# Fifty-six offsets in the last part of a list scheduler's order: soft-capped attention followed by a mixture of attention experts

## The chip, the core and the metric

The kernel runs on one core of a Trainium2 chip. A core has five engines that run side by side, each with its own in-order stream of instructions: TensorE (PE in the profile: matrix products and transposes, with weight loads shown apart as PEld), VectorE (DVE), ScalarE (ACT), GpSimd (POOL) and SyncE (SP), which here issues nearly all DMAs. Sixteen DMA engines move data between the device memory and the on-chip buffer. TensorE writes into eight banks of accumulators; the other engines read results from there. The metric is the device time of one execution in microseconds; the figure given for a kernel is the median of its runs.

## The reference

The first stage is attention for 8 batches and 12 heads, with 448 positions and a head size of 64, whose scores are capped by a tanh:

```python
scores = scale * np.matmul(q, k.transpose(0, 1, 3, 2))
scores = cap * np.tanh(scores / cap)
attn = softmax(scores)
x = (attn @ v) with heads merged        # 8 x 448 x 768
```

The second stage is a layer of four experts, each of them a causal attention with a head of size 64. A gate picks two of the four for every position:

```python
logits = x @ w_gate
w = softmax over the two largest logits
for e in range(4):
    q, k, v = x @ wq[e], x @ wk[e], x @ wv[e]
    a = softmax(causal(scale * q @ k.T))
    out += (weight of e at this position) * (a @ v @ wo[e])
```

The output is 8 x 448 x 768 in 32-bit floats.

## The kernel before

The first stage goes by pairs of heads: 48 pairs, six to a batch, and two more groups (numbers 48 and 49) that hold the last 128 query rows of the last batch for three pairs each. For each pair, TensorE turns q and k around, forms the scores in a left group of three banks (X) and a right group of two (Y), ScalarE takes tanh from there in three pieces (line 854) and then the exponential in place (line 866). TensorE multiplies the result with v (lines 881 and 889), VectorE normalises (lines 910 and 913), and the result is turned around into the tile xT, by TensorE for the early pairs and by a transposing DMA (line 400) for later ones.

The second stage for a batch runs while the first stage of the next batch goes on. Its parts, by the names that the scheduler gives them:

- `v6_n` (line 1003): values and gate logits of batch 6 for four blocks of 128 rows; `k6_r`, `q6_r` (line 1011): its keys and queries for two pairs of experts.
- The gate: a chain of small GpSimd operations on the logits, which ends in masks `mB6` that a DMA turns around into `mT`. VectorE multiplies the queries by them (`qm6`, line 1085).
- `sB6_s` (line 1207): the causal scores of the s-th chosen expert, 18 products in seven pieces; ScalarE takes their exponential (`eB6_s`, line 1216), GpSimd cuts the diagonal blocks (line 1226).
- `pvB6_s` (line 1266): scores times values, for four row blocks; VectorE scales them into `oB` (line 1281), GpSimd adds the two choices (line 1291), DMAs turn the sum around into `oT`, and `wo6` (line 1328) multiplies by the output weights, in two halves per row block. A copy by VectorE or ScalarE (line 388) puts each half into an output tile `ob`, and SP stores it (line 1342) when both halves are there.

Batch 7 has nothing to hide behind. Its first 320 rows are done by `last` (lines 1431 to 1513) and its last 128 rows by `last2` (lines 1593 to 1651): products of halves that were begun earlier (`hkL`, `hqL`), the other halves (`kL`, `qL`, line 1443), values (`vL`, `cvL`, line 1476), scores (`sL..`, line 1495, and `sR.`, line 1624), products with the values (`pvL0` to `pvL2`, line 1533, and `pvL3`, line 1651), normalisation (lines 1357 to 1365), transposes (`oTL`, line 1372), output products (`woL`, line 1394), copies into the tiles `kf`, and five stores (lines 1403, 1409 and 1412). Two of the last stores are issued by ScalarE's queue, the others by SP.

None of this order is written out. The kernel first records every operation in a graph, with an engine, an estimated duration and what it reads and writes. `dues` gives each operation a due time, worked back from the fixed sequence of ScalarE's tanh and exponential operations. `solve` then is a list scheduler: at each step it finds, for each engine, the operation that can start first by the estimates, and among those that can start at about that moment it takes the one with the smallest rank. The rank is the due time plus some corrections:

```python
d = u.due + lag if u.first or left < TAIL else max(u.due + lag, t0 + 0.0)
d -= 7.653 * (u.grp is not None and not u.opens and left >= TAIL)
```

A table of seeds, one for each 4 us of the planner's time, adds a small pseudo-random shift. Banks are given out in the same pass, so another order also means other banks. After that the operations are issued engine by engine in the order found; at run time each engine works through its list in order, and waits where an input or a bank isn't ready. An operation that may run on VectorE or ScalarE (`alt`) is placed on either only when the fixed ScalarE sequence is over.

Of the kernel before, what the change touches and what calls it, by code (L numbers as in the profile page):

```python
# [21 lines left out]
FLIGHT = 8  # L22
JIT = 1.798
SEEDS = (0, 0, 110, 0, 0, 306, 0, 782, 317, 0, 303, 0, 680, 715, 825, 0, 899, 21, 0, 595, 84, 0, 0, 430, 634, 477, 0, 0, 952, 0, 477, 0, 829, 206, 468, 485, 0, 0, 522, 517, 134, 0, 182, 0, 903, 141, 149, 0, 334, 0, 875, 527, 0, 0, 667, 121, 852, 28, 0, 742, 969, 79, 85, 225, 0, 0, 0, 500, 463, 0, 0, 356, 833, 724, 418, 803, 322, 931)
TWIRE = 0.1
BEGIN = {"POOL": 0.8, "DVE": 0.9, "SP": 0.8, "ACT": 0.8, "PE": 1.25}
NWARM = 6
# [31 lines left out]
class Graph:  # L59
# [79 lines left out]
    def solve(self, when, banks, lent):  # L139
        free = dict(BEGIN)  # L140
        sent = []
        ready = {}
        at = {}
        bank_at = {b: 0.0 for b in (*banks, *lent)}
        taken = {b: [o for o in self.ops if b in o.takes] for b in lent}
        for o in self.ops:
            o.nd = len(o.deps)
            if o.grp is not None:
                o.grp.bank = None
            if o.nd == 0:  # L150
                ready.setdefault(o.eng, []).append(o)
                at[o.idx] = 0.0
        order = []
        n = len(self.ops)
        left = sum(o.fixed for o in self.ops)
        half = 0
        lag = 0.0
        wire = 0.0

        def pick(o, t):  # L160
            best = None
            for b in o.grp.banks:
                s = max(t, bank_at[b])
                if s >= INF:
                    continue
                if b in taken and taken[b]:
                    continue
                if best is None or s < best[0]:
                    best = (s, b)
            return best or (INF, None)  # L170

        def est(o, e):
            t = max(free.get(e, 0.0), at[o.idx])
            if o.opens:
                t = pick(o, t)[0]
            for b in o.takes:
                t = max(t, bank_at[b])
            if (e == "SP" or o.wire) and len(sent) >= FLIGHT:
                t = max(t, sent[-FLIGHT])
            if e == "PE" and o.half != half:  # L180
                t = max(t, free.get(e, 0.0) + SWITCH)
            return t

        while len(order) < n:
            best = None
            for e, rs in ready.items():
                if not rs:
                    continue
                c = [(est(o, e), o) for o in rs if e == o.eng or not left]
                if not c:  # L190
                    continue
                t0 = min(x[0] for x in c)
                if t0 >= INF or (best is not None and t0 >= best[0]):
                    continue
                def rank(x):
                    u = x[1]
                    if u.name[:4] == "gexp":
                        return -INF, 0.0, 0
                    d = u.due + lag if u.first or left < TAIL else max(u.due + lag, t0 + 0.0)
                    d -= 7.653 * (u.grp is not None and not u.opens and left >= TAIL)  # L200
                    k = SEEDS[int(t0 / 4.0)] if t0 < 4.0 * len(SEEDS) else 0
                    if k:
                        d += ((u.idx * 40503 + k * 9973) % 1009 / 1009.0 - 0.5) * JIT
                    return d - 5.546 * (u.half == 1 and half == 1), u.due, u.idx

                near = t0 + (0.085 if left >= TAIL else SWITCH + 0.02)
                t, o = min((x for x in c if x[0] <= near), key=rank)
                early = e == "POOL" and t < HEAD
                if (e in ("PE", "DVE") or early) and not o.first:
                    for t2, u in c:  # L210
                        if u.first and u.due + lag < t + o.occ + 0.517 and t2 < t + (
                                o.occ if early else max(SWITCH + 0.01, min(o.occ, 0.25))):
                            t, o = t2, u
                            break
                if best is None or t < best[0]:
                    best = (t, e, o)
            assert best is not None, "stuck"
            t, e, o = best
            ready[o.eng].remove(o)
            if o.alt:  # L220
                ready[o.alt[0]].remove(o)
                if e != o.eng:
                    o.eng, o.occ, o.lat = o.alt
            left -= o.fixed
            o.start = t
            if e == "PE" and t < WARM:
                o.lat = 2.0 * o.base
                free[e] = t + 2.0 * o.base
                o.lat += 0.165
            else:  # L230
                free[e] = t + o.occ
            if o.wire:
                wire = max(wire, t + (LAND if t > 3.0 else LAND0)) + o.wire
                o.lat = wire - t + (0.35 if t > 3.0 else 0.0)
            if o.eng == "SP" or o.wire:
                sent.append(t + o.lat)
            if e == "PE":
                half = o.half
            if o.idx in when:
                lag = t - when[o.idx]  # L240
            if o.opens:
                b = pick(o, t)[1]
                o.grp.bank = b
                bank_at[b] = INF
            for b in o.takes:
                bank_at[b] = INF
                if b in taken:
                    taken[b].remove(o)
            if o.closes:
                bank_at[o.grp.bank] = t + o.lat + SEM  # L250
            for b in o.frees:
                bank_at[b] = t + o.lat + SEM
            order.append(o)
            for s, late in o.succ:
                at[s.idx] = max(at.get(s.idx, 0.0), t + self.gap(o, s, late))
                s.nd -= 1
                if s.nd == 0:
                    ready.setdefault(s.eng, []).append(s)
                    if s.alt:
                        ready.setdefault(s.alt[0], []).append(s)  # L260
        return order
# [19 lines left out]
def kernel(  # L281
# [116 lines left out]
    def turned(n, dst, src, r, w, name, due=None):  # L398

        sp(lambda: nc.sync.dma_start_transpose(  # L400
            dst().rearrange("p (n t) -> p n t", t=128), src()), r, w, due, name,
           wire=TWIRE * n, occ=1.25)

# [1385 lines left out]
```

## Time and profile before

| | |
|---|---|
| time, median of 3 runs | 304.8 us (304.11 to 304.95) |
| profiled execution: span | 303.4 us |
| difference of the median to that span | 1.4 us |
| busy share of PE / DVE / ACT / POOL | 93% / 72% / 96% / 61% |
| instructions in the profile | 8986 |

The profiler gives the profiled execution as a span, from its first to its last instruction; a time of its own beside the span is not given, so the median of the runs stands for it. Busy time of TensorE is modelled, since its products are pipelined: the step from one product's start to the next one's is a better measure of what it costs than its listed duration. In a view in order of time each line has the start, the duration, the engine, the line of the kernel, the operation, what it writes and reads, and how many alike are merged; square brackets hold idle time ahead of it and what ended that. A "q" behind an engine's name is its queue, where DMAs are issued.

### The profile page before, as it was taken

How to read it: one execution, taken by the hardware profiler on the slowest of the kernel's cores; microseconds unless marked ns; L12 is line 12 of the kernel's file. 1: busy time of each engine (PE TensorE's matmuls, PEld its weight loads, DVE VectorE, ACT ScalarE, POOL GpSimd, SP SyncE). 2: the span in 40 equal slices, each digit the busy share in tenths (PEclk: the TensorE clock that was granted, in tenths of full speed). 3: DMA queues.
4: the chain of work that ended last, by engine and by line, in shares of the span. 5: the costliest groups of instructions: out<-in, count | busy, mean ns of one | idle time of the engine just before them, and what ended most of it. 6: DMA issues, size and time to landing. Idle time of an engine off the chain costs nothing.

```text
span 303.4 us, 8986 instructions
## 1 busy us (share of the span) xinstructions
PE 281.0 (93%) x3488; PEld 187.7 (62%) x3488; DVE 218.2 (72%) x653; ACT 290.8 (96%) x247; POOL 184.7 (61%) x515
## 2 busy tenths in 40 slices
PE   7779789899999999999999999999999999999993
PEld 3445546477665776667675776557566565676861
DVE  3336558577877878597877877788777758678993
ACT  5999999999999999999999999999999999999792
POOL 6793433998699684958589553945569212940340
PEclk9999999999999999999999999999999999999998
DMA  6789979999971999568997972178026730433327
GB/s 192 181 200 292 238 200 274 259 256 224 251 168 56 283 269 248 144 180 251 228 245 139 269 218 81 37 140 235 3 55 130 216 79 2 94 75 127 98 88 278
DMA packets 86875, 53.13 MB, mean 175 GB/s; under 512 B 47536, under 2 KB 83120, under 8 KB 86832
## 3 DMA queue, kind: packets, MB, share of 16 engines
q1 hardware_dynamic: 86448, 52.13, 68.1%
q8 instruction: 27, 0.44, 0.6%
q10 hardware_dynamic: 384, 0.43, 0.4%
q14 instruction: 16, 0.13, 0.2%
HBM read 36.19 MB, written 11.01 MB: 156 GB/s over the span
## 4 chain that ended last, share of the span: by engine, by line
ACT 59%; PE 30%; issue 3%; DMA 3%; DVE 2%; SPq 1%; POOL 1%; POOLq 0%; ACTq 0%
ACT yp L854 29%; ACT yp L866 25%; PE A L1011 4%; ACT pP L1216 4%; PE A L889 3%; PE Y L801 3%; PE A L1328 3%; DMA kf<-in_k_dram 2%; PE A L1003 2%; PE A L1266 2%; PE A L881 2%; PE X L1207 1%; PE A L934 1%; PE X L801 1%; DMA oT<-oS 1%
## 5 line engine op out<-in xcount | busy, mean ns | idle before, releaser
L866 ACT ACTIVATE yp<-yp 128x3136 f16<-128x3136 f16 (+4 forms) x51 | 141.1, 2769 | 0.0
L854 ACT ACTIVATE yp<-Y 128x896 f16<-128x896 f32 (+2 forms) x100 | 99.2, 992 | 1.2 <-PE Y L801 1.2
L854 ACT ACTIVATE yp<-X 128x1344 f16<-128x1344 f32 (+2 forms) x50 | 67.1, 1343 | 0.6 <-PE X L801 0.4
L889 PE MATMUL A<-v,yp 128*128 128x65 f16 x1116 | 55.4, 193 | 0.0
L889 PEld LDWEIGHTS <-yp 128*128 128x128 f16 x1116 | 48.4, 97 | 3.7 <-issue 1.5
L881 PE MATMUL A<-vtz,yp 128*128 128x130 f16 x186 | 41.2, 222 | 4.4 <-ACT yp L866 2.7
L913 DVE TENSOR_TENSOR xk<-A,rca 128x256 f16<-128x256 f32 x96 | 39.9, 415 | 3.2
L691 POOL CAST v<-vf 128x384 f16<-128x384 f32 x48 | 24.0, 507 | 16.9 <-PE A L889 12.8
L655 POOL CAST q<-qf 112x512 f16<-112x512 f32 x44 | 26.7, 616 | 10.8 <-PE A L705 6.2
L764 DVE COPY qk<-A 128x960 f16<-128x960 f16 x32 | 20.5, 655 | 12.1 <-PE A L705 11.7
L881 PEld LDWEIGHTS <-yp 128*128 128x128 f16 x186 | 18.0, 97 | 17.8 <-issue 8.5
L388 DVE COPY ob<-A 128x384 f32<-128x384 f32 (+1 forms) x48 | 25.2, 551 | 4.7 <-PE A L1328 4.3
L910 DVE RECIPROCAL rca<-A 128x4 f32<-128x4 f32 x96 | 17.0, 178 | 15.3 <-PE A L889 13.9
L801 PE MATMUL Y<-qk 64*128 64x448 f16 x136 | 24.7, 358 | 2.3 <-ACT yp L854 1.4
L1281 DVE SCALAR_TENSOR_TENSOR oB<-A,rcb,mw 128x256 f16<-128x256 f32 x53 | 24.9, 480 | 1.8
L1266 PE MATMUL A<-vB,pP 128*128 128x260 f16 x132 | 22.5, 274 | 1.7 <-DVE oB L1281 1.6
L1328 PE MATMUL A<-wo,oT 128*128 128x384 f16 x98 | 22.4, 325 | 1.0 <-DMA oT<-oS 0.5
L1291 POOL TENSOR_TENSOR oS<-oB,oB 128x512 f16<-128x512 f16 x14 | 16.0, 1153 | 10.6 <-issue 9.5
L1003 PE MATMUL A<-wvg,xT 128*128 128x260 f16 x168 | 22.1, 274 | 0.4 <-DVE vB L999 0.3
L705 PE MATMUL A<-ident,q 112*128 112x112 f16 x192 | 19.9, 213 | 1.2 <-POOL q L655 1.1
L640 POOL CAST k<-kf 128x384 f16<-128x384 f32 x33 | 16.3, 509 | 6.3 <-DMA kf<-in_k_dram 3.1
L1226 POOL TENSOR_SCALAR_AFFINE_SELECT pP<-pP 128x384 f16<-128x384 f16 x14 | 7.4, 525 | 20.6 <-ACT pP L1216 20.6
(240 smaller groups left out, 598.7 us busy)
## 6 DMA issues: line engine op xcount, KB each, us to landing
qf<-in_q_dram SPq DMA_DIRECT2D x23, 448.0 KB, 6.0
kf<-in_k_dram SPq DMA_DIRECT2D x23, 384.0 KB, 4.9
vf<-in_v_dram SPq DMA_DIRECT2D x23, 384.0 KB, 5.2
out_dram<-ob SPq DMA_DIRECT2D x21, 384.0 KB, 3.3
ktf<-in_k_dram SPq DMA_DIRECT2D x46, 32.0 KB, 4.8
vtf<-in_v_dram SPq DMA_DIRECT2D x46, 32.0 KB, 4.8
out_dram<-ob SPq DMA_DIRECT2D x6, 192.0 KB, 2.9
ob<-in_moe_wv_dram SPq DMA_DIRECT2D x2, 384.0 KB, 4.9
```

Of the source, the lines that this page charges most:

```text
L388: (nc.scalar.copy if o.eng == "ACT" else nc.vector.tensor_copy)(dst(), src())
L655: e(q16[i], qf[s][:, h].rearrange("p h (c d) -> p c h d", c=QC))
L801: nc.tensor.matmul(dst[:, g, o], kT[r, 128 * (c + 1) : 128 * (c + 2)], t[r, qs], start=True, stop=True,)
L854: ACTS[what, p] = act(c_act(n * (b - a)), lambda: nc.scalar.activation(y[:, a:b, 0:n], src[:, 0 : b - a, 0:n], AF.Tanh, scale=isc / capf), ...
L866: act(c_act(n * (b - a), False), lambda a=a, b=b, n=n: nc.scalar.activation(y[:, a:b, 0:n], y[:, a:b, 0:n], AF.Exp, scale=capf), ks, ks, f ...
L881: nc.tensor.matmul(ps[:, n, :, :], y[:, 2 * S + w : 2 * S + w + 128], vtz[u], start=(n == 0), stop=False, skip_group_check=True,)
L889: nc.tensor.matmul(ps[:, n, h, :], y[:, o : o + 128], v16[u][:, h, c, :], start=False, stop=(c == 2), skip_group_check=True,)
L913: dve(c_dve(128 * m), lambda g=g, i=i, rc=rc, m=m: nc.vector.tensor_tensor(xk[p % NXK][:, 2 * i : 2 * i + m, :, :], view(g)[:, 0:m, :, 0:D ...
L1003: nc.tensor.matmul(bank(g)[:, 0 : E * Dh + E], xT[x][:, j, WIN[n] : WIN[n] + 128], wvg[:, j, :], start=(j == j1), stop=(j == jn),)
L1266: nc.tensor.matmul(bank(g)[:, 0 : E * (Dh + 1)], pB[pi][:, o : o + 128], vB[x][:, c, :, :], start=(t == 0), stop=(t == len(cs) - 1),)
L1281: dve(c_dve(E * Dh) + 0.06, lambda g=g, k_=k_, n=n: nc.vector.scalar_tensor_tensor(oB[s][:, n, :, :], view(g)[:, :, 0:Dh], rcb[k_][:, 0, : ...
L1328: nc.tensor.matmul(bank(g)[:, 0 : D // 2], oT[x][:, n // 2, r, n % 2, :], wo2[r][:, c0:c1], start=(r == 0), stop=(r == 1),)
```

## The change

A table gives 56 operations, named by their number in the graph, an offset in hundredths of a microsecond. From 249.5 us of the planner's time on, the offset is added to the operation's rank; a positive one lets others go first. Nothing else is changed.

```diff
+RANKS = (
+    (249.5, {
+        2260: -386, 2303: -114, 2314: 197, 2330: 2378, 2341: 324, 2348: 3565, 2372: 3326, 2399:
+        -428, 2401: -1930, 2484: 214, 2490: -459, 2508: 5066, 2519: 291, 2526: -4288, 2529:
+        -162, 2566: 232, 2568: 1338, 2569: -246, 2575: 354, 2583: 806, 2586: 1059, 2591: 749,
+        2593: 434, 2604: 113, 2607: 115, 2608: 79, 2632: 192, 2647: 153, 2648: 2441, 2655: 1463,
+        2663: 275, 2665: -730, 2678: 187, 2680: 644, 2689: 2077, 2692: -456, 2694: 1630, 2695:
+        6618, 2696: -2260, 2724: 343, 2725: 98, 2729: 835, 2732: -33, 2734: 418, 2739: 765,
+        2744: 384, 2746: -1204, 2768: 842, 2773: 182, 2774: 799, 2784: 320, 2787: 206, 2789:
+        767, 2794: 829, 2802: 704, 2807: -322,
+    }),
+)
...
                     d = u.due + lag if u.first or left < TAIL else max(u.due + lag, t0 + 0.0)
                     d -= 7.653 * (u.grp is not None and not u.opens and left >= TAIL)
+                    for since, table in RANKS:
+                        if t0 >= since:
+                            d += table.get(u.idx, 0) / 100
```

The numbers that matter below: 2330 is the start of `k6_0` and 2348 of `q6_1`; 2372 is a row block of `pvB5_1`; 2508 is the fourth of the seven pieces of the scores `sB6_0`; 2526 is a row block of `pvB6_0`; 2583, 2586, 2591 and 2593 are halves of the output products `wo6` (2583 is the second half of row block 0); 2689 and 2692 are value blocks `vL`; 2695 and 2696 are the value block `cvL`; 2746 is a transpose `oTL`.

What the offsets do to the order, from the listing of both programs: up to the planner's 249.5 us all engines' lists are the same. Behind that, `k6_0` moves behind `q6_0`; the logits and values `v6_0` move from the last place of four to the third; three `wo5` halves and most of `pvB6` move ahead; the seven pieces of `sB6_0` are split after the third, with two groups of pair 44 and a block of `pvB5_1` between. In the last part two of the four score blocks `sL..` move ahead of the last attention groups, the two value blocks `vL` change places, and the last row blocks' products are interleaved. The last nine stores, seven of them on SP, come there in the order ob0, ob2, kf0, ob1, kf2, kf1, kf3 instead of ob0, ob1, ob2, kf0, kf3, kf1, kf2 (kf2 and kf3 have a second half on ScalarE's queue).

## The prediction

> **What bounds the kernel now.** I read the page's totals, then the chain that ended last, then each engine in order of time over the last 50 us (the change acts from 249.5 us of the planner's time), then the stretches of the end with their DMA share.
>
> ```profile
> span 303.4 us, 8986 instructions
> PE 281.0 (93%) x3488; PEld 187.7 (62%) x3488; DVE 218.2 (72%) x653; ACT 290.8 (96%) x247; POOL 184.7 (61%) x515
> ```
>
> ScalarE carries the kernel: tanh and exp stand back to back. The part that the change touches, by stretch (busy us of each engine with its count, then granted clock, DMA share, GB/s):
>
> ```profile
> core 0: us, PE busy (x) PEld busy (x) DVE busy (x) ACT busy (x) POOL busy (x), PEclk, DMA share, GB/s
> 265.00:275.00 10.00, 9.39 (x143) 7.16 (x142) 7.96 (x28) 9.62 (x10) 4.03 (x13) 1.00 0.47 135
> 284.90:290.00 5.10, 5.07 (x78) 3.87 (x76) 4.75 (x22) 2.65 (x10) 1.06 (x2) 1.00 0.23 51
> ```
>
> Until 284.9 us ScalarE sets the pace, with TensorE nearly as full; behind it ScalarE is half idle, and TensorE and VectorE carry a chain of small products and copies. Then come the stores. The same view, cut finer at the end:
>
> ```profile
> 293.80:294.80 1.00, 1.00 (x15) 0.75 (x15) 0.86 (x4) 0.70 (x4) 0.54 (x2) 1.00 0.95 378
> 294.80:295.20 0.40, 0.40 (x4) 0.12 (x3) 0.40 (x2) 0.40 (x3) 0.00 (x0) 1.00 0.18 69
> 295.20:296.00 0.80, 0.80 (x17) 0.66 (x16) 0.73 (x4) 0.80 (x3) 0.00 (x0) 1.00 1.04 422
> 299.00:300.00 1.00, 0.00 (x0) 0.00 (x0) 0.00 (x0) 0.09 (x1) 0.00 (x0) 1.00 1.04 409
> 300.00:301.00 1.00, 0.00 (x0) 0.00 (x0) 0.00 (x0) 0.00 (x0) 0.00 (x0) 1.00 0.88 215
> 293.80:302.00 8.20, 4.75 (x47) 2.71 (x46) 4.47 (x15) 3.73 (x10) 0.54 (x2) 0.99 0.92 336
> 302.00:303.40 1.40, 0.00 (x0) 0.00 (x0) 0.00 (x0) 0.00 (x0) 0.00 (x0) 0.50 0.00 0
> ```
>
> This is the reading on which the forecast turns. From 293.8 to 302.0 the 16 DMA engines are busy 0.92 of the time: 8.20 x 0.92 = 7.54 us of transfers, with one real hole at 294.8 to 295.2. So the end is set by a queue of stores that never empties, and the last copy only decides when the last piece joins it. The stores, by issue and by size:
>
> ```profile
> 292.94 2.68 SPq L1342 DMA_DIRECT2D out_dram<-ob  x3
> 296.05 0.33 SPq L1412 DMA_DIRECT2D out_dram<-kf  x1
> 299.12 0.53 ACTq L1409 DMA_DIRECT2D out_dram<-kf  x1
> out_dram<-ob SPq DMA_DIRECT2D x3, 384.0 KB, 2.8
> out_dram<-kf SPq DMA_DIRECT2D x2, 384.0 KB, 3.3
> out_dram<-kf ACTq DMA_DIRECT2D x2, 192.0 KB, 3.0
> out_dram<-kf SPq DMA_DIRECT2D x2, 192.0 KB, 2.8
> ```
>
> Nine stores, 5 x 384 + 4 x 192 = 2688 KB, all issued between 292.94 and 299.12. The first data move 0.86 us after the first issue (293.80 - 292.94), and 1.36 us pass from the last data (302.0) to the end of the span. So the span is 292.94 + 0.86 + 8.20 + 1.36 = 303.36. The median of the runs, 304.8, is 1.4 us above the span; I carry that difference over unchanged.
>
> **The change, part by part.** No operation is added or taken away; 56 offsets change which ready operation the planner takes. Listing both programs by engine, the first difference stands at TensorE's blocks for pair 42; from there the counts are the same but for one copy that goes from ScalarE to VectorE.
>
> *Scores of expert block 6 (offset +50.66 on the fourth of their seven pieces).* Before, all 18 products stand together and end just as ScalarE gets free; ScalarE then loses 0.38 us once, behind a wait of TensorE for a transposing DMA:
>
> ```profile
> 265.25 1.08 PE L1207 MATMUL X<-qm,kB 128*128 128x64 f16 x18
> 266.72 0.22 PE L881 MATMUL A<-vtz,yp 128*128 128x130 f16 x1
> 266.96 0.22 PE L881 MATMUL A<-vtz,yp 128*128 128x130 f16 x1
> 267.20 0.49 PE L1266 MATMUL A<-vB,pP 128*128 128x260 f16 x3
> 269.00 0.82 PE L1328 MATMUL A<-wo,oT 128*128 128x384 f16 x4 [0.47 <-DMA oT<-oS]
> 266.44 1.07 ACT L1216 ACTIVATE pP<-X 128x1024 f16<-128x1024 f32 x1
> 273.40 1.13 ACT L854 ACTIVATE yp<-X 128x1152 f16<-128x1152 f32 x1 [0.38 <-PE X L801]
> ```
>
> In the new order two attention groups (0.24 each, 266.72 to 266.96) and three L1266 products (0.11 each) stand between the pieces: 0.48 + 0.33 = 0.81 us later, less some 0.25 by which TensorE gets there earlier, since the two blocks of the q products no longer wait behind the late k block. ScalarE waits 0.56 us there. In return the waits of 0.47 and 0.38 should go: in the new program the sum L1291 that feeds this oT stands ahead of part of the gate work on GpSimd, the logits that start the gate chain come one block earlier, and so SP's queue (masks, xT, oT, in the same order) moves up. The price of a transpose that lands later is bounded by nothing and by the 3.34 us of this row of the chain, against 2.3 to 2.4 for most of its kind:
>
> ```profile
> 265.62 3.34 DMA oT<-oS
> ```
>
> At 3.34 us it would still land before its products. Sum for ScalarE's chain: +0.56 - 0.38 = +0.2, less for work that closes up later; I take +0.1, between -0.4 (no wait at the scores) and +0.6 (the waits stay).
>
> *The tail: the first store.* From the last attention group of TensorE to the second product of output block 0, which completes the first store, it is 291.29 - 285.29 = 6.00 us:
>
> ```profile
> 285.29 0.22 PE L960 MATMUL X1s<-vtz,yp 128*128 128x130 f16 x1
> ...
> 285.53 0.28 PE L1593 MATMUL A<-xT,wq 128*128 128x128 f16 x2
> 285.64 0.28 PE L1593 MATMUL A<-xT,wk 128*128 128x128 f16 x2
> ...
> 287.45 0.31 PE L1495 MATMUL X2s<-qB,kB 64*128 64x320 f16 x1
> ...
> 287.73 0.27 PE L1593 MATMUL A<-xT,wk 128*128 128x128 f16 x2
> ...
> 291.05 0.25 PE L1495 MATMUL A<-qB,kB 64*128 64x192 f16 x1
> ...
> 291.29 0.50 PE L1328 MATMUL X1s<-wo,oT 128*128 128x384 f16 x2
> ...
> 292.18 0.48 PE L1328 MATMUL X2s<-wo,oT 128*128 128x384 f16 x2
> 292.50 0.29 PE L1533 MATMUL A<-vB,pP 128*128 128x65 f16 x4
> 292.36 0.55 DVE L388 COPY ob<-X1s 128x384 f32<-128x384 f32 x1
> ```
>
> In the new order that product comes later: ahead of it now stand two more L1328 pairs (0.32 each, 292.18 to 292.50), the 24 products of L1533 (four take 0.13 up to the next group, so 0.78) a score block (0.24, 291.05 to 291.29) and two pairs of 128 columns (0.11 each, 285.53 to 285.64), while two score blocks (0.28, 287.45 to 287.73, and 0.24) have moved ahead of the start and four changes between half-height and full-height products go (some 0.1 each). That is 0.64 + 0.78 + 0.24 + 0.22 - 0.52 - 0.40 = +0.96. Its copy stood 1.07 us after it (292.36 - 291.29), behind other VectorE work; the shortest this can be is the product's own 0.50 and a little more, about 0.62. I take 0.45 off, since fewer gate operations stand there, and 0.1 for a pair that leaves the start. First store: +0.1 + 0.96 - 0.45 - 0.1 = +0.5, bounded by 0 and +1.4; I take +0.4.
>
> *The tail: the last store.* ScalarE waits twice for TensorE ahead of its last copies:
>
> ```profile
> 297.77 0.48 ACT L388 COPY kf<-X1s 128x384 f32<-128x384 f32 x1 [0.61 <-PE X1s L1394]
> 298.61 0.48 ACT L388 COPY kf<-A 128x384 f32<-128x384 f32 x1 [0.37 <-PE A L1394]
> ```
>
> In the new order the products of all four last blocks are interleaved, so that one block's copies run beside another's products; the two waits, 0.98 us, go, and about half a microsecond of TensorE's own waits with them. The last issue should go from 299.12 to some 297.6, an estimate between no gain and 2 us. It does not enter the sum, because what stands behind it is the queue of stores.
>
> *The drain.* 7.54 us of transfers stay, since the bytes do. The hole at 294.8 to 295.2 (0.4 x 0.82 = 0.33) goes: in the new SP order the second store stands right behind the first with its copies done. Of the 0.12 lost in 300.0 to 301.0 I count all; the ramp at both ends stays. So the drain is 8.20 - 0.45 = 7.75, bounded by 7.54 and 8.20.
>
> [...] The rows show SP and ACT stores drawing on the same busy share (1.04 at 299 to 300, with a store of ACT's queue issued at 299.12). [...]
>
> *Sum.* +0.4 (first store) - 0.45 (drain) = -0.05 us: a span of 303.3, and 304.7 us beside the median of 304.8.
>
> **The rivals.** *Faster: the stores give way too.* For it: the tail work does end about 1.5 us earlier, and the stretch at 300 to 301 moves only 215 GB/s at a share of 0.88; if this half-rate store overlaps with others instead of standing at the end, 0.45 goes. With that, and the first store no later than now: -0.45 - 0.45 = -0.9, 303.9; with ScalarE's chain 0.4 earlier as well, 303.5, which I take as its time. Without any sharing of engines it would be the last issue 1.5 earlier, 303.3. Against it: 2688 KB at the 400 GB/s of the full rows need most of 7 us, whatever the order.
>
> *Slower: VectorE's queue before the first store.* VectorE is busy 4.75 of 5.10 us there and gains a copy (0.55). If the copy of the second half of block 0 again stands 1.07 us behind its product, and the row of normalisations that now comes earlier costs two more copies (2 x 0.55) ahead of it, the first store is 0.4 + 0.45 + 1.1 = 1.95 later and the time is 304.8 + 1.95 - 0.45 = 306.3. It decides once that copy starts more than 1.35 us after the present 292.36. For it: the store needs both halves, and SP's queue is in order, so everything waits behind it. Against it: VectorE's gate chain for the last rows, which held the copy until 292.36, moves up.
>
> *The waits at the scores stay and grow:* ScalarE +0.6, first store +0.9, 305.3. This lies within the range. That the table does nothing is excluded by the listing of the new program.
>
> **How the numbers follow.** A measurement of this kernel can tell about 0.3% (0.9 us) from no change. Forecast (within that) 0.57, with the 305.3 of the grown waits counted there; faster 0.25; slower by VectorE's queue 0.18. The predicted time is 304.7. The range goes from 303.5, the faster rival's own time, to 305.7, half way into the slower one; about 0.1 is left out on each side.
>
> **What would show it.** Right: the first store of ob at 293.2 to 293.5, the last store issued before 298, a DMA share near 1.0 from about 294.2 with no hole, data until about 302; ScalarE with a gap of about 0.5 ahead of the L1216 exp near 266.9 and none of 0.38 at 273; no TensorE wait for oT. Wrong: if data end before 301.2, the stores do not set the end as I read them; if the first store is later than 294, the order of the copies is at fault; a TensorE wait for mT or oT beyond 0.5 us would shift all of it.

## The result, and the profile after

The changed kernel takes 306.83 us (median of 9 runs, 306.56 to 308.84) beside 304.8 us of the kernel before (9 runs on the same chip): a ratio of 1.0063, with a 95% interval of 1.0034 to 1.0091. It is slower by about 2 us, where 304.7 us and no change were forecast.

Line numbers of the new kernel are 15 higher (L1216 is now L1231). The page's totals, after:

```profile
span 305.4 us, 8987 instructions
PE 281.7 (92%) x3488; PEld 188.4 (62%) x3488; DVE 219.0 (72%) x654; ACT 290.6 (95%) x246; POOL 184.6 (60%) x515
```

The busy times move by 0.8 us at most, so most of the 2.0 us between the two spans is idle time. The stretches of the end (busy us of each engine with its count, then granted clock, DMA share, GB/s):

```profile
265.00:275.00 10.00, 9.96 (x147) 7.37 (x144) 8.80 (x29) 9.62 (x11) 3.14 (x9) 1.00 0.56 123
...
293.80:294.80 1.00, 1.00 (x18) 0.74 (x18) 0.97 (x4) 0.95 (x3) 0.41 (x1) 1.00 0.00 0
294.80:296.00 1.20, 1.20 (x17) 0.88 (x14) 0.94 (x5) 1.05 (x3) 0.00 (x0) 1.00 0.76 307
297.00:298.00 1.00, 0.92 (x6) 0.32 (x4) 0.90 (x3) 0.50 (x3) 0.00 (x0) 1.00 1.05 411
299.00:300.00 1.00, 0.00 (x0) 0.00 (x0) 0.00 (x0) 0.00 (x0) 0.00 (x0) 1.00 0.98 224
300.00:301.00 1.00, 0.00 (x0) 0.00 (x0) 0.00 (x0) 0.00 (x0) 0.00 (x0) 1.00 1.03 332
302.00:303.00 1.00, 0.00 (x0) 0.00 (x0) 0.00 (x0) 0.00 (x0) 0.00 (x0) 0.63 0.61 226
303.00:304.00 1.00, 0.00 (x0) 0.00 (x0) 0.00 (x0) 0.00 (x0) 0.00 (x0) 0.50 0.10 35
295.10:304.06 8.96, 2.82 (x21) 1.36 (x18) 2.92 (x8) 2.29 (x6) 0.00 (x0) 0.90 0.86 308
```

The first row is for later. The others show three things. Data start 1.30 us later (295.10, before 293.80). At 299 to 300 the DMA engines are all busy, yet move only 224 GB/s. And the end is ragged: from 302 on the share falls to 0.61 and 0.10: some of the 16 engines have finished and others have not. In the kernel before, the last stretch with data was this, and nothing came behind it:

```profile
301.00:302.00 1.00, 0.00 (x0) 0.00 (x0) 0.00 (x0) 0.00 (x0) 0.00 (x0) 0.91 0.74 246
```

The stores of the kernel after, in order of issue:

```profile
294.25 0.83 SPq L1357 DMA_DIRECT2D out_dram<-ob  x2
295.33 0.33 SPq L1427 DMA_DIRECT2D out_dram<-kf  x1
296.26 0.33 SPq L1357 DMA_DIRECT2D out_dram<-ob  x1
297.24 0.49 SPq L1424 DMA_DIRECT2D out_dram<-kf  x1
297.24 0.52 ACTq L1424 DMA_DIRECT2D out_dram<-kf  x1
297.93 0.67 SPq L1427 DMA_DIRECT2D out_dram<-kf  x1
298.47 0.71 ACTq L1418 DMA_DIRECT2D out_dram<-kf  x1
298.69 1.10 SPq L1418 DMA_DIRECT2D out_dram<-kf  x1
```

The last store is issued 0.43 us earlier than before (298.69, before 299.12), but the span ends 6.7 us behind it where it was 4.2. The two stores of L1424 have 64 rows each, half of the 128 partitions. They ended the queues before; now they stand in the middle.

One more difference must be taken out before the two profiles are compared. The engines' lists are the same up to the first exp of expert block 5, and there the new profile is already 0.31 us late. In order of time, the kernel before and then the kernel after:

```profile
243.50 1.18 ACT L1216 ACTIVATE pP<-X 128x1024 f16<-128x1024 f32 x1
```

```profile
243.81 1.17 ACT L1231 ACTIVATE pP<-X 128x1024 f16<-128x1024 f32 x1
```

In the profiles of the experiments this row comes between 242.51 and 246.35, and where I followed it back it arose in the first 30 us of an execution. So below every trace is read from that exp on: from it to the end of the last instruction it is 59.86 us in the kernel before and 61.55 after, a difference of 1.69.

### The profile page after: what moved, and what is told of

Read it like the earlier page. It is cut to its first block, busy times and chain, and to the rows that moved or that the text cites. A ratio compares the mean times of both kernels' runs of the same rounds, so it can differ in the third digit from the quotient of the medians.

```text
span 305.4 us, 8987 instructions
## 1 busy us (share of the span) xinstructions
PE 281.7 (92%) x3488; PEld 188.4 (62%) x3488; DVE 219.0 (72%) x654; ACT 290.6 (95%) x246; POOL 184.6 (60%) x515
## 4 chain that ended last, share of the span: by engine, by line
ACT 56%; PE 33%; DVE 3%; issue 3%; DMA 1%; ACTq 0%; POOL 0%; DVEq 0%; POOLq 0%
ACT yp L869 28%; ACT yp L881 24%; PE A L1026 4%; PE A L904 4%; ACT pP L1231 4%; PE Y L816 4%; PE A L1343 3%; PE A L896 2%; PE A L1018 2%; PE A L1281 2%; PE X L1222 2%; PE X L816 1%; PE A L949 1%; DMA ktf<-in_k_dram 1%; DVE xk L928 1%
## 5 line engine op out<-in xcount | busy, mean ns | idle before, releaser
L928 DVE TENSOR_TENSOR xk<-A,rca 128x256 f16<-128x256 f32 (+1 forms) x96 | 39.8, 416 | 3.2
L925 DVE RECIPROCAL rca<-A 128x4 f32<-128x4 f32 (+1 forms) x96 | 17.1, 178 | 15.7 <-PE A L904 14.4
L1343 PE MATMUL A<-wo,oT 128*128 128x384 f16 x102 | 23.4, 326 | 0.5 <-DVE qm L1100 0.4
```

The source lines that it names most:

```text
L928: dve(c_dve(128 * m), lambda g=g, i=i, rc=rc, m=m: nc.vector.tensor_tensor(xk[p % NXK][:, 2 * i : 2 * i + m, :, :], view(g)[:, 0:m, :, 0:D ...
L1343: nc.tensor.matmul(bank(g)[:, 0 : D // 2], oT[x][:, n // 2, r, n % 2, :], wo2[r][:, c0:c1], start=(r == 0), stop=(r == 1),)
```

## The experiments

All results together. "From the exp" is the time from the first exp of block 5; the drain runs from the first to the last data of the stores. "Above count" compares the last data with a count from the issue times: data 0.86 us behind the issue, one store behind the other, 0.965 us for a store of 384 KB, 0.575 for 192 KB in 128 short rows, 0.9 for 192 KB in 64 rows. The first and the last of these times are 407 and 218 GB/s, beside rows at 409 to 422 and at 215 to 224; the short rows take some 0.07 us each, taken here as eight to an engine. Time and ratio come from all runs of a kernel, the four columns behind them from one trace each.

| run | time, us | ratio to before | from the exp: first store | from the exp: end | drain | above count |
|---|---|---|---|---|---|---|
| before | 304.8 | 1 | 49.44 | 59.86 | 8.19 | 0.0 |
| after | 306.83 | 1.0063 (1.0034 to 1.0091) | 50.44 | 61.55 | 8.96 | 1.2 |
| a_halves_last | 305.86 | 1.0032 (1.0005 to 1.0059) | 50.52 | 60.51 | 7.71 | -0.1 |
| a_no_2583 | 305.77 | 1.0024 (1.0003 to 1.0044) | 48.35 | 60.42 | 9.78 | 0.4 |
| a_no_halves | 305.05 | 1.0007 (0.9981 to 1.0033) | 50.44 | 59.39 | 6.73 | 0.7 |
| a_one_half | 305.33 | 1.0009 (0.9984 to 1.0034) | 50.44 | 60.15 | 7.45 | 0.6 |
| a_halves_sp | 306.45 | 1.0054 (1.0026 to 1.0082) | 50.44 | 61.71 | 9.11 | 1.3 |
| a_scores_together | 306.6 | 1.0053 (1.0022 to 1.0085) | 50.56 | 61.66 | 8.94 | 1.2 |
| a_one_store | 312.63 | 1.0246 (1.0193 to 1.0299) | 50.43 | 67.26 | 14.62 | - |
| a_quarters | 305.65 | 1.0045 (1.0028 to 1.0063) | 50.44 | 60.40 | 7.91 | - |
| b_first_second | 305.69 | 1.0019 (0.9997 to 1.0041) | 50.53 | 60.51 | 7.71 | -0.1 |
| b_halves_ahead | 306.41 | 1.0037 (1.0014 to 1.006) | 49.28 | 61.23 | 9.79 | 0.8 |
| b_one_store | 311.88 | 1.0211 (1.0157 to 1.0266) | 49.34 | 66.88 | 15.31 | - |
| b_quarters | 304.9 | 1.0002 (0.9987 to 1.0016) | 49.39 | 59.81 | 8.13 | - |

Names with a_ are edits of the kernel after, names with b_ of the kernel before. The kernel before took 304.76 to 305.23 us beside them. The end from the exp and the ratio (0.01 is 3.05 us) tell the same within the interval, but for a_quarters: there the trace is 0.54 us behind the kernel before and the ratio says 0.85 to 1.9.

**Is it the place of the two 64-row stores?**

```diff
     order = G.solve(when, AUX, XB + YB)
+    order.sort(key=lambda o: o.name == "sthL")
```

> The kernel after, with the two 64-row stores of its third last block (L1424) moved behind every other store on their queues; the order of all other work is the same. Theory Q (order of the queue): in the kernel after these two stores stand in the middle of the queue, move at 224 GB/s (299 to 300 us) and send the 16 DMA engines out of step, so that the last data come at 304.06 where the first came at 295.10, 8.96 us for 7.79 us of transfers. At the end of the queue, as in the kernel before, the drain should be 7.9 to 8.3 us again: span 305.4 - 0.7 to 1.0, time 305.8 to 306.1. Rival R (backlog alone): the engines run apart because the stores are issued faster than they drain, whatever their order: 306.6 to 307.1. The first store is issued at 294.1 to 294.4 by both.

```profile
297.72:305.43 7.71, 2.81 (x21) 1.35 (x18) 2.92 (x8) 2.28 (x6) 0.00 (x0) 1.00 0.95 358
```

This row of the stretches is the whole drain. With the same operations, bytes and first store, it takes 7.71 us at a share of 0.95 where the kernel after took 8.96 at 0.86. The end comes 1.04 us earlier and the time is 305.86: theory Q. The backlog alone (R) is out, since the stores are issued at the same rate. The intervals of the two ratios overlap, so this rests on the traces, read from the exp. There the three kernels whose stores stand in the order of the kernel after (itself, a_halves_sp and a_scores_together) end within 0.16 us of one another.

**The same turned round, in the kernel before.** The full store ahead of them is moved behind them:

```diff
     order = G.solve(when, AUX, XB + YB)
+    order.append(order.pop([o.idx for o in order].index(2741)))
```

> The kernel before with its second 128-row store of L1412 (kf_79) moved behind SP's 64-row store, so that the two 64-row stores no longer end the queue; all else is the same. Counted by the rates of the rows, the queue runs empty for 0.5 us ahead of the 64-row stores and the end comes 0.5 later: 305.3. Theory Q (64-row stores ahead of other stores send the engines out of step, 1.1 us in the kernel after): 1.3 to 1.7 later, 306.1 to 306.5, and the last engine ends over 0.8 us behind the median one. Rival R (the backlog in the kernel after does that, not the place): 305.0 to 305.5, with the engines within 0.4 us of each other as in the kernel before.

```profile
301.00:302.00 1.00, 0.00 (x0) 0.00 (x0) 0.00 (x0) 0.00 (x0) 0.00 (x0) 0.55 0.81 304
302.00:302.44 0.44, 0.00 (x0) 0.00 (x0) 0.00 (x0) 0.00 (x0) 0.00 (x0) 0.50 0.21 84
```

The end comes 1.37 us later from the exp and the ratio gives 1.13, against 0.5 expected for the empty stretch alone. The last data stand 0.8 us above the count, and the end is ragged again (share 0.81, then 0.21), though less than in the kernel after. Theory Q holds in both kernels.

**How much without them?** All 64-row stores left out, and then one of them:

```diff
     order = G.solve(when, AUX, XB + YB)
+    order = [o for o in order if o.name != "sthL"]
```

> The kernel after without its two 64-row stores (L1424), so that 128 output rows are not written; all else is the same. Theory Q: 384 KB of 2688 are not moved, at the 224 GB/s that they have there 1.7 us, at full rate 0.95, and the engines stay in step (0.5 to 0.7 us): 304.3 to 305.4. Theory L (the last copy and its store set the end, stores overlap): the last issue stays at 298.7 and the last store lands 2.7 to 3.2 us later as in the kernel before, or all stays: 306.0 to 306.8. The span's end minus the last issue tells: 6.7 us in the kernel after, 4.2 in the kernel before.

```diff
     order = G.solve(when, AUX, XB + YB)
+    order = [o for o in order if (o.name, o.eng) != ("sthL", "ACT")]
```

> The kernel after without the 64-row store of ACT's queue (64 output rows are not written); the one of SP's queue stays in the middle. Counted by the rates of the rows (384 KB in 8 x 121 ns a engine, 192 KB of short rows in 0.575 us, 192 KB of 64 rows in 0.9 us, one behind the other), the drain is 8.0 - 0.9 = 7.1 us; what comes above that is engines out of step (1.1 us in the kernel after, 0.8 with both such stores left out, nearly nothing with both at the end). Theory F (one slow store in the middle is enough): 8.0 to 8.2 us of drain, time 305.7 to 306.0. Theory P (only the pair, lower and upper half in flight together): 7.1 to 7.9, time 304.8 to 305.5. The span from the first exp of block 5 to the end, 61.55 in the kernel after, tells it without the differences of the start.

The last stretches, of the run without both stores and then of the run without one:

```profile
300.40:301.13 0.73, 0.00 (x0) 0.00 (x0) 0.00 (x0) 0.00 (x0) 0.00 (x0) 1.00 0.06 23
```

```profile
301.70:302.20 0.50, 0.00 (x0) 0.00 (x0) 0.00 (x0) 0.00 (x0) 0.00 (x0) 0.50 0.24 89
```

These two runs leave 128 and 64 output rows unwritten. Their ends come 2.16 and 1.40 us earlier; leaving out one store of 192 KB is worth more than its 0.9 us, as the expectation of the pair (P) said. But the first row corrects theory Q: with no 64-row store at all, a share of 0.06 for 0.73 us is one engine of sixteen that is late. So they don't bring all of the disorder. Some 0.6 to 0.7 us of it is there without the pair, and the pair in the middle adds some 0.5. Where the pair ends the queue, none of it is left (table: 0.0, -0.1, -0.1). 
What makes one engine late can be read from the traces. In each of the fourteen, one packet of 8 KB that the view of the DMA queues lists as "instruction" stands among the stores. In the run without both 64-row stores the view from 296.64 to 296.95 has it (packets, MB, share of the 16 engines):

```profile
q14 instruction: 1, 0.01, 6.2%
```

That share is one engine for the whole 0.31 us. The two rows that follow it take 0.24 and 0.36 us where others take 0.12, so some 0.67 us are lost. Each store ends with sixteen packets of 4 bytes, taken here as one to an engine. By their times, no engine of this run ends a store more than 0.2 us behind all others ahead of that packet, and in each store behind it one engine does, by 0.65 to 0.80 us. The trace doesn't name the engines: that it is the same one is inferred, since the times join within 0.02 us. The late engine is in the kernel before too. In the run b_halves_ahead one engine works alone until the 64-row stores have data:

```profile
298.14:298.84 0.70, 0.00 (x0) 0.00 (x0) 0.00 (x0) 0.00 (x0) 0.00 (x0) 1.00 0.06 24
```

In the kernel before, the last full-height store ends on fifteen engines by 300.30 and on one at 300.96, but each of the two 64-row stores behind it ends on all sixteen within 0.33 us. So a pair at the end lets the late engine catch up. Why it can is argued: the rows of the pair may not be limited by the engines. No run took the instruction packet away.

**Two queues or one?** Both 64-row stores on SP's queue:

```diff
-                eng = nc.scalar if r0 else nc.sync
+                eng = nc.sync
```

> The kernel after with both 64-row stores on SP's queue, one behind the other, at the same place; ACT's queue keeps only its last store. Theory 2Q (two queues at once: rows of ACT's store among those of SP's send the engines out of step): the engines end within 0.5 us of each other and the drain is 8.0 to 8.3: 306.0 to 306.2. Theory F (form of the rows): slow rows as before, 1.6 us for the pair, drain 8.6 to 9.0: 306.5 to 307.0.

The drain is 9.11 us, a little above the range of theory F, and the time 306.45: the second queue is not the cause.

**Why is a 64-row store slow?** First all 128 rows in one store, written as two groups of 64 in the output:

```diff
-                sp(lambda eng=eng, r0=r0, r1=r1, bb=bb, t0_=t0_: eng.dma_start(out[bb, t0_ : t0_ + 64, :], o[r0:r1, :]),
+                sp(lambda: nc.sync.dma_start(out.rearrange("b t d -> (b t) d")[2816:3456].rearrange("(a r) d -> a r d", a=2)[:, 256:320, :], o),
...
     order = G.solve(when, AUX, XB + YB)
+    order = [o for o in order if (o.name, o.eng) != ("sthL", "ACT")]
```

> The kernel after, with its two 64-row stores (192 KB each, L1424) joined into one store of all 128 rows (384 KB) on SP's queue at the place of the first; the output is the same. Theory F (form): a row of a 64-row store takes 215 to 227 ns where a row of a 128-row store takes 121, so 128 rows x 0.1 us / 16 engines = 0.8 us of engine time goes (7.71 to 6.9), and the engines stay in step; the drain falls from 8.96 to 7.0 to 7.4 us: 305.0 to 305.3. Theory P (place alone: what the run with the two stores at the end gained, 1.0 us, is all that there is): a store in the middle holds the queue up whatever its form, no gain: 306.6 to 306.9.

> The same edit on the kernel before: one 128-row store of 384 KB in place of the two 64-row stores that end its queues. Theory F: the 0.8 us of slow rows at 300 to 302 go; the last store is issued at 299.1 as now and lands 2.4 to 2.9 us later where it took 3.2: 304.0 to 304.5. Theory P: the last store's own issue and landing bound the end here, 304.7 to 304.9. Both orders of the tail then have the same bytes at the same rate, and what is left between this run and the one before it in the list is the later first store.

```profile
305.00:310.00 5.00, 0.00 (x0) 0.00 (x0) 0.00 (x0) 0.00 (x0) 0.00 (x0) 0.50 0.13 52
```

Both kernels lose 6 to 7 us, by neither theory. In the row (kernel after with this edit) the share is 0.13, which is 2 of 16 engines, for 5 us: the outer dimension of this store is 2, and two engines carry it all at 52 GB/s. The run told nothing on the slow rows. That the outer dimension set the number of engines is inferred from this one form of store, which ran at 2 engines where the stores at 298 to 299 in the kernel after keep all 16 busy (share 1.04).

Then four stores of 32 rows, in turn from the two queues, in both kernels:

```diff
-                sp(lambda eng=eng, r0=r0, r1=r1, bb=bb, t0_=t0_: eng.dma_start(out[bb, t0_ : t0_ + 64, :], o[r0:r1, :]),
+                sp(lambda eng=eng, r0=r0, bb=bb, t0_=t0_: [eng.dma_start(
+                    out[bb, t0_ + i : t0_ + i + 32, :], o[r0 + i : r0 + i + 32, :]) for i in (0, 32)],
```

> The kernel before with each of its two last stores (64 rows, one on SP's and one on ACT's queue) cut into two of 32 rows; same rows, same queues, same place. So far a row of these stores takes up to 227 ns where a row of a 128-row store takes 121. Theory H (half the rows' partitions at a time: the 16 DMA engines all read the same half of SBUF's partitions, and the lower and the upper half come one after the other): with the pieces issued in turn by two queues, engines that work on the lower half run beside engines that work on the upper one, and of the 1.8 us that the two stores take (300.2 to 302.0) up to 0.8 goes: 304.0 to 304.5, if two more issues (0.35 us each) do not eat it. Rival (a small store is slow by itself, whatever runs beside it): 304.7 to 305.3, with two more issues and two more landings.

> The same edit on the kernel after, where these stores stand in the middle of the queue. Theory H: rows at 121 ns again for the most part and engines less out of step; the drain falls from 8.96 to 7.6 to 8.4 us: 305.5 to 306.3. Rival (small stores are slow by themselves): drain 8.9 to 9.3, 306.7 to 307.2.

The kernel before with this edit, and then the kernel after with it:

```profile
300.00:301.00 1.00, 0.00 (x0) 0.00 (x0) 0.00 (x0) 0.00 (x0) 0.00 (x0) 1.00 0.98 297
301.00:302.00 1.00, 0.00 (x0) 0.00 (x0) 0.00 (x0) 0.00 (x0) 0.00 (x0) 1.00 0.51 194
```

```profile
294.68:302.59 7.91, 2.82 (x21) 1.36 (x18) 2.92 (x8) 2.29 (x6) 0.00 (x0) 0.90 0.93 349
```

The rate is as theory H has it: 297 GB/s at 300 to 301, where the kernel before had 215. In the kernel before nothing comes of it (304.9, where theory H had 304.0 to 304.5): the share falls to 0.51 in the last stretch, since a few engines end late. In the kernel after the drain falls from 8.96 to 7.91 us, inside the 7.6 to 8.4 expected, and the time is 305.65. So smaller pieces of the two halves in turn were faster here, and small stores were not slow by themselves. That half of the partitions limits a 64-row store (215 and 224 GB/s, where the four stores had 297) fits this, but no view names the partitions in flight, so it stays a theory.

**What is the first store worth?** In the kernel before it is delayed, by storing the second block first; in the kernel after it is brought forward, by dropping one entry:

```diff
     order = G.solve(when, AUX, XB + YB)
+    s0, s1 = [i for i, o in enumerate(order) if o.name == f"st{LB - 1}"][:2]
+    order.insert(s1, order.pop(s0))
```

> The kernel before with its first two stores of ob swapped in SP's queue: nothing is stored until the second block is copied, so that the first issue moves from 292.94 to 294.3 and the other of the two follows at once; copies, products and all later stores stay. Theory Q: the drain begins 1.37 us later and loses the hole of 0.33 us at 294.8 to 295.2, so the end comes 1.0 us later: 305.8. Theory L (the last copies set the end): 304.8, no change. If the queue has slack of its own ahead of the last stores, something between, which is the share of the first store's lateness that reaches the end.

```diff
-        -162, 2566: 232, 2568: 1338, 2569: -246, 2575: 354, 2583: 806, 2586: 1059, 2591: 749,
+        -162, 2566: 232, 2568: 1338, 2569: -246, 2575: 354, 2586: 1059, 2591: 749,
```

> The kernel after without the entry 2583 of its table (the second product of output block 0 of expert block 6): that product stands right behind the first again, two stores keep their places, and the first is issued some 2 us earlier (292.1 to 292.3 where it was 294.25), the second some 0.1 later than the first was, the last some 0.4 to 0.6 later. Theory Q (a queue of stores that sets the end): 384 KB leave early and 2304 KB remain from the second store on, 8.96 x 2304 / 2688 = 7.68 us, begun 0.6 later than now, so 0.7 us less: 306.1. Theory L (the last copy sets the end): 307.2 to 307.4. If only the time of the first store counts: 304.8.

```profile
294.63:302.34 7.71, 3.39 (x32) 1.84 (x30) 3.25 (x11) 2.67 (x7) 0.00 (x0) 0.92 0.96 358
```

```profile
293.80:295.20 1.40, 1.40 (x22) 0.96 (x21) 1.37 (x5) 1.31 (x4) 0.41 (x1) 1.00 0.06 14
```

In the kernel before (first row) a first store that is 1.09 us later from the exp moves the end by 0.65, since the empty stretch behind it goes: 7.71 us of drain. That is something between the two theories, nearer to the queue. This run and a_halves_last have the same first store (50.53 and 50.52), the same drain and the same end (60.51), with quite different work ahead. In the kernel after (second row) the early store is followed by 1.4 us of almost nothing (share 0.06), and still the end comes 1.13 earlier, more than the 0.7 expected. The last data stand 0.4 us above the count there, against 1.2 in the kernel after; why the engines are less out of step is not shown.

**Does the wait at the scores cost anything?**

```diff
     order = G.solve(when, AUX, XB + YB)
+    p = [o.idx for o in order].index(2484)
+    late = [o for o in order[p:] if o.name == "sB6_0"]
+    order = order[:p] + late + [o for o in order[p:] if o not in late]
```

> The kernel after with the last pieces of the scores of expert block 6 put back behind the first ones, ahead of the two attention groups and the L1281 products that stood between; nothing else is moved. Theory S (ScalarE's chain carries it): the exp of these scores starts 0.5 us earlier against the exp of the block before (23.15 us after it where it was 23.67), the 0.5 stays until the last exp (e49) and the end: 306.3 to 306.5. Rival: the work that now comes later (the products for the sum of block 5, the attention group for pair 45) delays a transpose or a bank by as much, and e49 and the end stay: 306.7 to 307.0.

```profile
268.55 1.05 ACT L1231 ACTIVATE pP<-X 128x1024 f16<-128x1024 f32 x1
...
270.72 0.97 ACT L869 ACTIVATE yp<-X 128x960 f16<-128x960 f32 x1 [0.53 <-PE X L816]
```

The exp of the scores comes 0.53 us earlier from the exp of block 5 (268.55 - 245.40 = 23.15, in the kernel after 23.68), and two steps later ScalarE waits 0.53 us for TensorE, a wait that the kernel after does not have. The end from the exp moves by 0.11, the wrong way. Theory S falls: TensorE is full here (9.96 us of 10 in the kernel after), and what is put ahead in its list delays something else.

None of these twelve is faster than the kernel before, the two that write fewer rows included. By the count above, its stores follow one another without a gap from 296.15 on, and none of them waits more than 0.21 us for the one ahead, but for the second of the 64-row pair, which is issued with the first. So, by the count, moving a few stores earlier by more than that would only open a gap elsewhere.

## Why the prediction was wrong

The 2.00 us between the two spans, of one trace each, are 0.31 from the start of the execution, 0.65 from the later first store (b_first_second and a_halves_last against the kernel before) and 1.04 from the place of the 64-row stores (a_halves_last against the kernel after). The prediction had -0.05 for the second (first store +0.4, empty stretch and the rest of the drain -0.45) and nothing for the third.

*Scores.* The mechanism was right. The wait was put at 0.56 us and is 0.53 (by so much the exp comes earlier in the run with the scores together; the row below counts 0.38 as idle). The waits of 0.38 and 0.47 are gone, as forecast. In the kernel after, ScalarE and TensorE in order of time:

```profile
266.83 0.56 PE L1222 MATMUL X<-qm,kB 128*128 128x128 f16 x8
267.49 1.02 ACT L1231 ACTIVATE pP<-X 128x1024 f16<-128x1024 f32 x1 [0.38 <-POOL vB L1437]
267.82 0.82 PE L1343 MATMUL A<-wo,oT 128*128 128x384 f16 x4
```

The row names a GpSimd memset as what ended ScalarE's wait; the scores end at 267.39, about as late, and the run with the scores together, where the wait is gone, shows that it was them. The products with oT start without a wait. Not foreseen was a wait of TensorE for a bank, from the view of waits:

```profile
PE A L1026 <- DVE oB L1296: 0.5, 1, 0.5
```

It came at the key products, whose place the table changes, and ScalarE's next two tanh pieces stood 1.11 us apart where it was 0.86. Counted from the exp, the last attention group is 0.25 later, against +0.1 forecast: inside the bounds of -0.4 to +0.6.

*First store.* This term was too small: +1.00 us against +0.4, though inside its bounds of 0 to +1.4. Its own items gave +0.5; the step from there to +0.4 had no reason. The tail of the kernel after:

```profile
285.85 0.22 PE L975 MATMUL A<-vtz,yp 128*128 128x130 f16 x1
...
290.10 0.41 DVE L403 CAST qL<-X0s 128x256 f16<-128x256 f32 x1
...
290.56 0.48 PE L1343 MATMUL X0s<-wo,oT 128*128 128x384 f16 x2 [0.21 <-DVE qL L403]
...
292.92 0.28 PE L1387 MATMUL A<-ident,oB 128*128 128x128 f16 x2
293.04 0.49 PE L1343 MATMUL X2s<-wo,oT 128*128 128x384 f16 x2
...
293.64 0.55 DVE L403 COPY ob<-X2s 128x384 f32<-128x384 f32 x1
```

From the last attention group to the second product it is 7.19 us (293.04 - 285.85) where it was 6.00: +1.19, forecast +0.86 (0.96, less 0.1 for the pair that leaves the start). The 0.1 counted there for a change between half-height and full-height products is in the trace of before: 0.15 us from the last products of 64 rows to the next full-height one (290.02 to 290.17), where those of 64 rows stand 0.05 to 0.06 apart. The missing 0.33 are two items: 0.21 us of waiting for the bank that VectorE's copy of qL frees, behind gate work, and 0.12 for a pair of transposes (292.92 to 293.04) that was left out of the count. The copy stands 0.60 behind its product, where 0.62 was the bound and -0.45 was taken off: right. With +0.25 from the group, +1.19, -0.47 and +0.03 up to the issue, it comes to +1.00. At the end of the program only 0.65 of that shows, since the empty stretch (0.33) goes, as forecast.

*Last store.* Forecast at 297.6, measured at 298.69; as said it did not enter the sum.

*The drain* is the step that failed. "7.54 us of transfers stay, since the bytes do" and the bounds of 7.54 to 8.20 took the time of a queue as a matter of bytes, whatever the order. It is 8.96 us, outside those bounds. The 7.75 forecast is what the stores take with the 64-row pair last and no gap (7.71 twice). The change moves this pair into the middle: the order of the nine stores, listed with the change, has kf2 ahead of kf1 and kf3. No cost was put on that, although a row at 215 GB/s beside rows at 409 said that these stores were of another kind. Nor did it count the engine that is late by some 0.7 us (0.67 in the run without 64-row stores), as is inferred from the instruction packet: with the pair at the end this doesn't show (-0.1 to 0.0 above the count), with full-height stores at the end it does (0.7).

*The rivals.* The faster one hoped that the half-rate store would overlap with others once it no longer stood at the end; the opposite happened. The slower one gave 306.3, near the result, by a mechanism that did not occur: VectorE's copy was not late, TensorE's product was, and the drain grew. The one of the grown waits had the first store at +0.9, near the +1.00, but the waits did not grow. The test "first store later than 294" did fire, but put the fault at the order of the copies. *Stores of SP and ACT* on one busy share: the row named for this was ill chosen. The store that ScalarE's queue issued at 299.12 has its first data at 301.18, so the share of 1.04 at 299 to 300 is nearly all SP's. With the pair on one queue or on two the drain is 9.11 and 8.96 us, and the time 306.45 and 306.83.

## What to carry to other kernels

When a program ends in a queue of stores, count it by kind of store, not by bytes, with the times of its own traces: here 384 KB in 128 full rows took 0.965 us by the count, 192 KB in 64 rows 0.9, and 384 KB with an outer dimension of 2 cost 6 to 7 us more than the pair it replaced. See too which kind stands last: the same stores drained in 7.71 us with the 64-row pair at the end and in 8.96 with it in the middle. Compare two profiles from a point that both reach by the same instructions; differences of the start were here up to 2.85 us from the kernel before, more than the effect. Before a wait is taken off one engine, see whether the engine it waited for has time to spare: here TensorE had none (busy 9.96 us of 10), and a wait of 0.53 us stood two steps later.

## What the runs showed of the hardware that was not expected

- A store with an outer dimension of 2 ran on two of the sixteen DMA engines (share 0.13), at 52 GB/s, and cost 6 to 7 us more than the two stores that it replaced.
- Stores of 64 rows moved 215 and 224 GB/s at DMA shares of 0.88 and 0.98; the same rows in four stores of 32, issued in turn by two queues, 297.
- A single 8 KB packet of the kind "instruction" among the stores took one engine 0.31 us, and in a queue with no 64-row store one engine ended every later store 0.65 to 0.80 us behind the others. Queues that ended in the two 64-row stores came out within 0.1 us of the count.
